# First weights in other buffers, w2 prepared sooner, and three statistics tied to the tile ahead of them, in a kernel of LayerNorm, Fourier mixing and MLP

## The chip, the cores and the metric

The kernel runs on one core of a Trainium2 chip. A core has a matrix engine (TensorE, PE in the profile), two elementwise engines (VectorE, DVE, and ScalarE, ACT), a slower general one (GpSimd, POOL) and a queue that issues transfers (SyncE, SP). PEld is TensorE's loading of weights, which runs beside its matmuls. The metric is the device time of one execution in microseconds; smaller is better. The time before is the median of three runs.

## The reference

```python
x = A_x                                    # (1, 2048, 576)
xn = _layernorm(x, axis=-1)
a = einsum("bsd,ed->bse", xn, dft_hid_re)
b = einsum("bsd,ed->bse", xn, dft_hid_im)
y = einsum("ts,bse->bte", dft_seq_re, a) - einsum("ts,bse->bte", dft_seq_im, b)
h = maximum(einsum("bsd,df->bsf", xn, w1), 0)      # w1: 576 x 4608
return x + y + einsum("bsf,fd->bsd", h, w2)        # w2: 4608 x 576
```

## The kernel before

All products are made from float16 halves: `split` (L164, L165) writes a high half on ScalarE (`hi = s * src`, rounded) and a low half on VectorE (`lo = s * src - hi`), and each product is a sum of three matmuls. The scale `s` is a power of two found from the largest magnitude: for w1 in `max_w1` (VectorE, L98) and `power_w1` (through TensorE, L140 and L148, with VectorE at L145 to L155), for w2 from sums of magnitudes that ScalarE makes in `sum_w2` (L375), and `power_w2`.

The 2048 rows of x are 16 tiles of 128 rows, in four groups g of four. The 4608 hidden columns of the MLP are nine blocks b of 512, each with two w1 halves (four parts f of 128 columns) and two w2 halves. A tile t goes through these steps: `stats([t])` takes mean and variance on VectorE (two L182, one L185, a square root on ScalarE at L192, then six small steps at L193 to L204); `normalize(t)`, N, writes the normalized tile on VectorE (L224) and its float16 form on ScalarE (L225); `remainder(t)`, E, subtracts the two (L229, L232), on VectorE for tile 0 and on GpSimd for the others; `transposes(t)`, T, makes nine transposes on TensorE (L240) and copies them out of PSUM on ScalarE into xT (L245, L248).

In the MLP `mlp1` and `tile_by` multiply xT by w1 (L286): `tile_by` for one tile of 128 rows and some parts f, `mlp1` for a group of four tiles. `mlp1_out` takes two such results through relu and makes sums and halves for a seven-product form of the second product (L303 to L314), with a temporary in a buffer tagged "stage" (two of them). `mlp2` makes one of the seven products with w2 (L328) and adds it to the accumulators on VectorE (L334). `sums_w2` (L405 to L408) and `split_w2` prepare w2.

The raw weights of all blocks lie in a pool "raw" of two buffers. At the start, SP issues tile 0 of x, the two w1 halves of block 0, x up to tile 7, then the two w2 halves, which have to wait until the w1 in their buffers is split, and then x of tiles 8 to 15 behind them.

The order in which an engine runs its instructions is not that of the source. It is fixed at compile time: the framework goes through the traced instructions with its own estimates of their times, prefers what stands earlier in the source, and takes something later when that is ready first. `tc.issue_after(ins)` ties that order: what is traced inside it for the engine of `ins` is put behind `ins` in that engine's queue, with no wait on a semaphore. `weave` runs a generator of steps and puts other calls between them. `fill(n)` traces n matmuls whose result nobody uses; they keep TensorE active.

Around the change, the source goes through block 0 for tiles 0 to 7 by hand: statistics of a tile, N, E, T, then `tile_by` for the parts of w1 that are split. The w2 of block 0 is summed, scaled and split between `tile_by(5)` and `mlp2`. After that a loop over blocks and groups runs `mlp1`, `mlp1_out` and the `mlp2` of the step before, with the preparation of the next block taken from a list.

Of the kernel before, what the change touches and what calls it, by code (L numbers as in the profile page):

```python
# [8 lines left out]
F16 = mybir.dt.float16  # L9
F32 = mybir.dt.float32  # L10
BF16 = mybir.dt.bfloat16
I32 = mybir.dt.int32
AF = mybir.ActivationFunctionType
# [28 lines left out]
def kernel(  # L42
# [41 lines left out]
        nc.sync.dma_start(r, src)  # L84

    def load_w1(b, i, parts=1):
        r = raws["w1", b, i] = raw.tile([P, 2 * KT, P], F32, tag="raw", name=f"raw_w1_{b}_{i}")
        n = 2 * KT // parts
        for k in range(0, 2 * KT, n):
            nc.sync.dma_start(r[:, k : k + n], w1[b, i][:, k : k + n])  # L90
# [70 lines left out]

    def split(hi, lo, src, s):

        nc.scalar.activation(hi, src, AF.Copy, scale=s)  # L164
        nc.vector.scalar_tensor_tensor(lo, src, s, hi, ALU.mult, ALU.subtract)  # L165


# [7 lines left out]
    def stats(ts):  # L175

        n = len(ts)
        mv = small.tile([P, n, 2], F32, tag=f"mv{n}", name=f"mv{ts[0]}")
        sts = [small.tile([P, 2, 6], F32, tag="st", name=f"st{t}", bufs=4) for t in ts]
        for t, st in zip(ts, sts):  # L180
            for j in range(2):
                nc.vector.bn_stats(st[:, j, :], acc[t][:, j * EH : (j + 1) * EH])  # L182
                yield
        for i, st in enumerate(sts):
            nc.vector.bn_aggr(mv[:, i], st.rearrange("p a b -> p (a b)"))  # L185
            yield
        r0, u, r, sh = (
            small.tile([P, n], F32, tag=f"{a}{n}", name=f"{a}_{ts[0]}") for a in ("r0", "u", "r", "sh")
        )
        m, v = mv[:, :, 0], mv[:, :, 1]  # L190
        stt = nc.vector.scalar_tensor_tensor
        nc.scalar.activation(u, v, AF.Sqrt, bias=eps)  # L192
        nc.vector.reciprocal(r0, u)  # L193
        yield

        stt(u, v, EPS, r0, ALU.add, ALU.mult)
        yield
        nc.vector.tensor_tensor(u, u, r0, ALU.mult)
        yield
        nc.vector.tensor_scalar(u, u, -0.5 * SX, 1.5 * SX, ALU.mult, ALU.add)  # L200
        yield
        nc.vector.tensor_tensor(r, u, r0, ALU.mult)
        yield
        stt(sh, m, -1.0, r, ALU.mult, ALU.mult)  # L204
        for i, t in enumerate(ts):
            means[t], factors[t], shifts[t] = mv[:, i, 0:1], r[:, i : i + 1], sh[:, i : i + 1]

    def weave(steps, *others):

        others = list(others)  # L210
        for _ in steps:
            if others:
                others.pop(0)()
        for f in others:
            f()
# [3 lines left out]
    def normalize(t, eng=nc.vector):  # L219
        stage = dpool.tile([P, 5 * EH], F32, tag="d", name=f"xn{t}")  # L220
        xn = xns[t] = stage[:, :D]

        xs = xss[t] = stage[:, D : 2 * D].bitcast(F16)
        eng.tensor_scalar(xn, acc[t], means[t], factors[t], ALU.subtract, ALU.mult)  # L224
        nc.scalar.activation(xs[:, :D], acc[t], AF.Identity, bias=shifts[t], scale=factors[t])  # L225

    def remainder(t, eng):
# [127 lines left out]
    def power_w1(b, i):  # L355
        s, p = (t["w1", b][:, i : i + 1] for t in (sc, pw))
        if b > 1:
            power(s, p, mx["w1", b][:, i : i + 1])
        else:
            power_pe(s, p, mx["b", i])  # L360

    def split_w1(b, f):
        i, r = divmod(f, 2)
        if r == 0:
            w1s[b, i] = mlp.tile([P, 2, 2 * KT, P], F16, tag="w1s", name=f"w1s{b}_{i}", bufs=4)
        w, k = w1s[b, i], slice(r * KT, (r + 1) * KT)
        split(w[:, 0, k], w[:, 1, k], raws["w1", b, i][:, k], sc["w1", b][:, i : i + 1])

    def sum_w2(b, i):

        if i == 0:
            mx["w2", b], sc["w2", b], pw["w2", b] = cell("mw2"), cell("tw2"), cell("pw2")
        junk = mlp.tile([P, 5, GH], F32, tag="stage", name=f"j{b}_{i}").rearrange("p a b -> p (a b)")
        junk = junk[:, : 4 * EH].rearrange("p (q e) -> p q e", e=EH)
        nc.scalar.activation(  # L375
            junk, raws["w2", b, i], AF.Abs, scale=2.0**-10, accum_out=mx["w2", b][:, i : i + 1]
        )
# [23 lines left out]
    def sums_w2(b, i):  # L401
# [5 lines left out]
        tt(b22, b22, b11, ALU.subtract)  # L407
        tt(b21, b21, b22, ALU.subtract)  # L408

    def split_w2(b, i, c):  # L410
        if c == 0:
            w2s[b, i] = mlp.tile([P, 2, 7, EH], F16, tag="w2s", name=f"w2s{b}_{i}", bufs=4)
        w, r = w2s[b, i], raws["w2", b, i]
        src = (r[:, 1:], r[:, :2], r[:, 2:])[c]
        q = (slice(B11, B22 + 1), slice(T3, T1 + 1), slice(T4, T2 + 1))[c]
        split(w[:, 0, q], w[:, 1, q], src, sc["w2", b][:, i : i + 1])
# [11 lines left out]
    def prepare_w2(b):  # L428
        steps = [lambda: sum_w2(b, 0), lambda: sum_w2(b, 1), lambda: power_w2(b)]
        steps += [lambda i=i: (split_w2(b, i, 0), sums_w2(b, i)) for i in range(NQ)]  # L430
        for i in range(NQ):
            steps += [lambda: None] * 2
            steps += [lambda i=i, c=c: split_w2(b, i, c) for c in (1, 2)]
        return steps
# [29 lines left out]
    def tile_by(t, fs, ps, wk=WK):  # L464
        g, c = divmod(t, TG)
        for i in fs:
            mlp1_group(0, g, i, slice(c * P, (c + 1) * P), ps[i], wk)

    no = lambda: None
    N, E, T = normalize, remainder, transposes  # L470

    def fill(n, src=idle):

        for _ in range(n):
            nc.tensor.matmul(ps[3][:, :256], src[:, :P], src[:, :256], start=True, stop=True)
# [5 lines left out]
    max_w1(0, 1)  # L481
    E(0, V)
    power_w1(0, 0)
    fill(14)
    T(0)
    fill(10, xss[0])
    split_w1(0, 0)
    tile_by(0, (0,), ps, WK0)
    split_w1(0, 1)
    tile_by(0, (1,), ps)  # L490
    weave(stats([1]))
    fill(8, xss[0])
    N(1)
    E(1, GP)
    T(1)
    fill(8, xss[1])
    s23 = stats([2, 3])
    weave(s23, no, lambda: max_w1(0, 2), no, lambda: max_w1(0, 3), lambda: power_w1(0, 1))
    tile_by(1, (0, 1), ps)
    split_w1(0, 2)  # L500
    N(2)
    E(2, GP)
    tile_by(0, (2,), ps)
    tile_by(1, (2,), ps)
    T(2)
    split_w1(0, 3)
    N(3)
    E(3, GP)
    tile_by(0, (3,), ps)
    tile_by(1, (3,), ps)  # L510
    T(3)
    tile_by(2, (0, 1, 2, 3), ps)
    weave(stats([4, 5, 6, 7]))
    for t in (4, 5, 6, 7):
        N(t)
        E(t, GP)
    T(4)
    tile_by(3, (0, 1, 2, 3), ps)
    pq = ps2.tile([P, 2, 512], F32, tag="ps2", name="p1_0_1")
    qs = [pq[:, 0], pq[:, 1]]  # L520
    T(5)
# [1 line left out]
    mlp1_out(0, 0, 0, *ps[:2])  # L523
    T(6)
    tile_by(5, (0, 1), qs)
    w = prepare_w2(0)
    w[0]()
    w[1]()
    w[2]()
    mlp1_out(0, 0, 1, *ps[2:])  # L530
    T(7)
    tile_by(6, (0, 1), qs)
    w[3]()
    tile_by(7, (0, 1), qs)
    w[4]()
    mlp1_out(0, 1, 0, *qs)
    for f in w[5:]:
        f()
# [322 lines left out]
```

## Time and profile before

| what | value |
|---|---|
| median of three runs | 1299.07 us (1297.1 to 1301.87) |
| the profiled execution | 1298.02 us |
| its span | 1296.2 us |
| TensorE busy | 1273.9 us (98%) |
| VectorE busy | 979.0 us (76%) |
| ScalarE busy | 532.0 us (41%) |
| GpSimd busy | 33.7 us (3%) |
| granted TensorE clock, mean | 0.997 |
| first matmul with w1 (L286) | at 11.81 us |
| first matmul with w2 (L328) | at 60.03 us |

The busy share of TensorE is an average that hides the start: in the first 60 us it is busy for 47.7 us, and some of that is `fill`. The granted clock is 1.00 but for a stretch in 17 to 24 us, where it is 0.50. A row of the timeline gives the start and the duration of an instruction, or of a run of like ones ("x9"), and in brackets how long the engine stood idle before it and what ended that.

### The profile page before, as it was taken

The page shows a single profiled execution, that of the slowest core. Times are in us where ns is not written, and L with a number is a line of the kernel's source. Part 1 is how long each engine was busy: PE and PEld are TensorE (multiplying, and loading weights), DVE is VectorE, ACT ScalarE, POOL GpSimd, SP SyncE. Part 2 cuts the span into 40 slices and gives each one's busy share as a digit, 9 for nine tenths or more (in the row PEclk, how much of TensorE's full clock was granted, in tenths as well). Part 3 has the DMA queues.
Part 4 walks back from the last instruction along what each step waited for, and adds up shares of the span by engine and source line. Part 5 has one row for each costly group of instructions (what it writes and reads, how often), then busy time and mean ns, then how long its engine had stood idle before and what let it go on. Part 6 is the DMA issues. An engine that isn't in the chain of part 4 may idle for free.

```text
span 1296.2 us, 21742 instructions
## 1 busy us (share of the span) xinstructions
PE 1273.9 (98%) x9106; PEld 873.0 (67%) x9106; DVE 979.0 (76%) x1671; ACT 532.0 (41%) x794; POOL 33.7 (3%) x60
## 2 busy tenths in 40 slices
PE   8799999999999999999999999999999999999998
PEld 6565666666666666666666556677777777777777
DVE  8978887596696685875866985567678887878875
ACT  4834444353443443443533432244443333333332
POOL 2210000000000000000000000000000000000000
PEclk8999999999999999999999999999999999999999
DMA  6102222122132131231221322330024435343420
GB/s 240 42 1 70 77 71 89 50 90 86 50 104 71 43 110 58 69 104 50 90 86 49 102 72 86 104 137 17 2 74 156 141 115 167 103 139 121 139 84 19
DMA packets 38002, 112.75 MB, mean 87 GB/s; under 512 B 3984, under 2 KB 10640, under 8 KB 37904
## 3 DMA queue, kind: packets, MB, share of 16 engines
q1 hardware_dynamic: 37904, 111.36, 25.8%
q8 instruction: 71, 1.16, 0.4%
q14 instruction: 27, 0.22, 0.1%
HBM read 101.91 MB, written 9.44 MB: 86 GB/s over the span
## 4 chain that ended last, share of the span: by engine, by line
PE 87%; DVE 6%; ACT 2%; DMA 2%; issue 1%; SPq 0%; POOLq 0%; POOL 0%; ACTq 0%; DVEq 0%
PE p L286 29%; PE p L795 25%; PE p L328 25%; PE pd L694 8%; DVE acc L334 1%; DMA raw_d<-in_dft_dram 1%; DVE w2s L165 1%; DVE h L307 0%; DVE c_md L98 0%; ACT xT L245 0%; DVE h L314 0%; DMA f<-in_cre_dram 0%; DVE xn L224 0%; ACT f L622 0%; ACT w2s L164 0%
## 5 line engine op out<-in xcount | busy, mean ns | idle before, releaser
L286 PE MATMUL p<-xT,w1s 128*128 128x512 f16 (+1 forms) x2268 | 462.6, 356 | 1.1 <-ACT xT L245 1.1
L328 PE MATMUL p<-w2s,h 128*128 128x288 f16 x3024 | 394.8, 286 | 3.4 <-DVE acc L334 2.9
L328 PEld LDWEIGHTS <-h 128*128 128x128 f16 x3024 | 295.2, 98 | 104.9 <-issue 4.6
L286 PEld LDWEIGHTS <-w1s 128*128 128x128 f16 x2268 | 209.1, 98 | 203.4 <-issue 1.9
L795 PE MATMUL p<-R,cs 128*128 128x288 f16 x2688 | 329.4, 286 | 0.0
L795 PEld LDWEIGHTS <-cs 128*128 128x128 f16 x2688 | 263.0, 98 | 66.3
L334 DVE SCALAR_TENSOR_TENSOR acc<-p,c_ub,acc 128x576 f32<-128x576 f32 x252 | 204.0, 812 | 17.6 <-PE p L328 17.2
L164 ACT ACTIVATE cs<-c,sc_c 128x1024 f16<-128x1024 f32 x112 | 128.6, 1148 | 201.3 <-PE p L795 149.5
L307 DVE SCALAR_TENSOR_TENSOR h<-p,h 128x256 f16<-128x256 f32 (+1 forms) x144 | 79.8, 556 | 135.6 <-ACT h L306 135.5
L165 DVE SCALAR_TENSOR_TENSOR cs<-c,sc_c,cs 128x1024 f16<-128x1024 f32 x112 | 143.7, 1283 | 49.9 <-ACT cs L164 49.7
L306 ACT ACTIVATE h<-p 128x256 f16<-128x256 f32 (+1 forms) x144 | 69.5, 484 | 221.6 <-PE p L286 219.3
L313 ACT ACTIVATE h<-s 128x1024 f16<-128x1024 f32 x72 | 76.1, 1057 | 170.8 <-DVE s L311 170.7
L694 PE MATMUL pd<-dsp,xT 128*128 128x288 f16 x896 | 109.9, 286 | 1.7 <-DVE acc L334 1.7
L314 DVE TENSOR_TENSOR h<-s,h 128x1024 f16<-128x1024 f32 x72 | 88.1, 1223 | 28.2 <-ACT h L313 28.1
L694 PEld LDWEIGHTS <-xT 128*128 128x128 f16 x896 | 87.7, 98 | 24.0 <-issue 1.9
L801 DVE SCALAR_TENSOR_TENSOR o<-p,us_c,o 128x288 f32<-128x288 f32 x112 | 57.5, 513 | 20.5 <-PE p L795 20.3
L622 ACT ACTIVATE f<-f 128x1024 f32<-128x1024 f32 x64 | 66.6, 1041 | 4.7 <-DMA f<-in_cre_dram 4.7
L164 ACT ACTIVATE w2s<-raw_w,c_sw 128x576 f16<-128x576 f32 (+1 forms) x54 | 43.9, 849 | 26.4 <-DVE c_sw L397 20.5
L165 DVE SCALAR_TENSOR_TENSOR w2s<-raw_w,c_sw,w2s 128x576 f16<-128x576 f32 (+1 forms) x54 | 46.6, 918 | 7.6 <-ACT w2s L164 7.6
L303 ACT ACTIVATE s<-p 128x256 f32<-128x256 f32 x72 | 26.6, 370 | 24.3 <-PE p L286 24.3
L712 ACT ACTIVATE R<-pd,c_rho 128x288 f16<-128x288 f32 x48 | 23.8, 499 | 21.8 <-DVE T L706 12.1
L165 DVE SCALAR_TENSOR_TENSOR w1s<-raw_w,c_sw,w1s 128x640 f16<-128x640 f32 x36 | 31.4, 892 | 0.0
(98 smaller groups left out, 633.0 us busy)
## 6 DMA issues: line engine op xcount, KB each, us to landing
f<-in_cre_dram SPq DMA_DIRECT2D x32, 512.0 KB, 3.5
f<-in_cim_dram SPq DMA_DIRECT2D x32, 512.0 KB, 3.5
c<-in_cre_dram SPq DMA_DIRECT2D x32, 512.0 KB, 4.1
c<-in_cim_dram SPq DMA_DIRECT2D x32, 512.0 KB, 4.6
raw_w<-in_w_dram SPq DMA_DIRECT2D x17, 640.0 KB, 4.1
raw_w<-in_w_dram SPq DMA_DIRECT2D x18, 576.0 KB, 4.0
acc<-in_x_dram SPq DMA_DIRECT2D x16, 288.0 KB, 6.4
spill<-acc SPq DMA_DIRECT2D x16, 288.0 KB, 2.5
```

What stands on the lines that cost most here:

```text
L164: nc.scalar.activation(hi, src, AF.Copy, scale=s)
L165: nc.vector.scalar_tensor_tensor(lo, src, s, hi, ALU.mult, ALU.subtract)
L286: nc.tensor.matmul(ps[:, cols], w1s[b, i // 2][:, hl, i % 2 * KT + k], xT[g][:, kx, cols], start=(n == 0), stop=(n == len(WK) - 1),)
L306: nc.scalar.activation(hi, src, AF.Relu)
L307: stt(lo, src, 0.0, hi, ALU.max, ALU.subtract)
L313: order["s"] = nc.scalar.activation(hi, st[:, 1:], AF.Copy).ins
L314: order["lo"] = nc.vector.tensor_tensor(lo, st[:, 1:], hi, ALU.subtract).ins
L328: nc.tensor.matmul(ps[:, c], h[:, x, qa, c * P : (c + 1) * P], w[:, y, qb], start=first and i == 0 and j == 0, stop=i == NQ - 1 and j == 2 ...
L334: nc.vector.scalar_tensor_tensor(o, ps, us[b], o, ALU.mult, ALU.add)
L622: nc.scalar.activation(f, f, AF.Abs, scale=2.0**-10, accum_out=sums_c[:, n, q : q + 1])
L694: nc.tensor.matmul(ps[j], xT[g][:, kx, c * P : (c + 1) * P], dsp[j][:, hl, k], start=(n == 0), stop=(n == len(XK) - 1),)
L795: nc.tensor.matmul(ps, w[:, a, k], r[:, c, rq], start=first and k == 0 and j == 0, stop=k == HK - 1 and j == 2, skip_group_check=not first,)
```

## The change

Seven edits, all of them about block 0 and tiles 0 to 7:

1. The raw w1 of block 0 goes into the two "stage" buffers, so that the two raw buffers are free for its w2 from the start.
2. For block 0 `sum_w2` writes its unused elementwise result into the buffer that the split w2 will have, instead of a "stage" buffer.
3. `split_w1(0, 0)` stands ahead of the first `fill(14)`, and the copies of T(0) are tied behind its high half on ScalarE (`order["hi"]`).
4. The statistics of tile 1 are tied behind N(0) on VectorE (`order["n"]`), and those of tiles 2 and 3, with the maxima and VectorE's part of the scale of w1's second half, behind N(1).
5. One `fill(8)` reads the low half of w1's part 1 in place of tile 0.
6. T(2) and the first two parts of `tile_by(2)` stand ahead of the split of w1's part 2; `split_w1(0, 2)`, N(3), T(3) follow.
7. The five first steps of `prepare_w2(0)` stand earlier: the two sums ahead of the statistics of tiles 4 to 7, scale and first split ahead of T(5), the second half's first split ahead of T(7).

```diff
     def load_w1(b, i, parts=1):
-        r = raws["w1", b, i] = raw.tile([P, 2 * KT, P], F32, tag="raw", name=f"raw_w1_{b}_{i}")
+        pool, tag = (raw, "raw") if b else (mlp, "stage")
+        r = raws["w1", b, i] = pool.tile([P, 2 * KT, P], F32, tag=tag, name=f"raw_w1_{b}_{i}")
...
-        nc.scalar.activation(hi, src, AF.Copy, scale=s)
+        order["hi"] = nc.scalar.activation(hi, src, AF.Copy, scale=s).ins
...
-        eng.tensor_scalar(xn, acc[t], means[t], factors[t], ALU.subtract, ALU.mult)
+        order["n"] = eng.tensor_scalar(
+            xn, acc[t], means[t], factors[t], ALU.subtract, ALU.mult
+        ).ins
...
-        junk = mlp.tile([P, 5, GH], F32, tag="stage", name=f"j{b}_{i}").rearrange("p a b -> p (a b)")
-        junk = junk[:, : 4 * EH].rearrange("p (q e) -> p q e", e=EH)
+        if b:
+            junk = mlp.tile([P, 5, GH], F32, tag="stage", name=f"j{b}_{i}")
+            junk = junk.rearrange("p a b -> p (a b)")[:, : 4 * EH]
+            junk = junk.rearrange("p (q e) -> p q e", e=EH)
+        else:
+            new_w2(b, i)
+            junk = w2s[b, i][:, 0, :4]
...
+    def new_w2(b, i):
+        w2s[b, i] = mlp.tile([P, 2, 7, EH], F16, tag="w2s", name=f"w2s{b}_{i}", bufs=4)
...
-        if c == 0:
-            w2s[b, i] = mlp.tile([P, 2, 7, EH], F16, tag="w2s", name=f"w2s{b}_{i}", bufs=4)
+        if b and c == 0:
+            new_w2(b, i)
...
-    no = lambda: None
+    no, after = lambda: None, lambda: tc.issue_after(order["n"])
...
     power_w1(0, 0)
+    split_w1(0, 0)
     fill(14)
-    T(0)
+    with tc.issue_after(order["hi"]):
+        T(0)
     fill(10, xss[0])
-    split_w1(0, 0)
     tile_by(0, (0,), ps, WK0)
     split_w1(0, 1)
     tile_by(0, (1,), ps)
-    weave(stats([1]))
-    fill(8, xss[0])
+    with after():
+        weave(stats([1]))
+    fill(8, w1s[0, 0][:, 1, KT:].rearrange("p k f -> p (k f)"))
     N(1)
     E(1, GP)
     T(1)
     fill(8, xss[1])
-    s23 = stats([2, 3])
-    weave(s23, no, lambda: max_w1(0, 2), no, lambda: max_w1(0, 3), lambda: power_w1(0, 1))
     tile_by(1, (0, 1), ps)
-    split_w1(0, 2)
+    with after():
+        s23 = stats([2, 3])
+        weave(s23, no, lambda: max_w1(0, 2), no, lambda: max_w1(0, 3), lambda: power_w1(0, 1))
     N(2)
     E(2, GP)
+    T(2)
+    tile_by(2, (0, 1), ps)
+    split_w1(0, 2)
+    N(3)
+    E(3, GP)
     tile_by(0, (2,), ps)
     tile_by(1, (2,), ps)
-    T(2)
     split_w1(0, 3)
-    N(3)
-    E(3, GP)
+    T(3)
     tile_by(0, (3,), ps)
     tile_by(1, (3,), ps)
-    T(3)
-    tile_by(2, (0, 1, 2, 3), ps)
+    w = prepare_w2(0)
+    w[0]()
+    w[1]()
     weave(stats([4, 5, 6, 7]))
     for t in (4, 5, 6, 7):
         N(t)
         E(t, GP)
+    tile_by(2, (2, 3), ps)
     T(4)
     tile_by(3, (0, 1, 2, 3), ps)
+    w[2]()
+    w[3]()
...
     T(6)
     tile_by(5, (0, 1), qs)
-    w = prepare_w2(0)
-    w[0]()
-    w[1]()
-    w[2]()
     mlp1_out(0, 0, 1, *ps[2:])
+    w[4]()
     T(7)
     tile_by(6, (0, 1), qs)
-    w[3]()
     tile_by(7, (0, 1), qs)
-    w[4]()
     mlp1_out(0, 1, 0, *qs)
```

## The prediction

> **What bounds the kernel now.** I read the page's engine shares first, then a table by stage, then the queues in order of time. The page: TensorE is busy in 1273.9 of 1296.2 us and the 40 slices show nines from the third slice on, so whatever can be won lies in the first 60 us, where this change is. Stage table of ten microseconds (columns: stretch, its length, busy time and instruction count of each engine, granted clock, DMA share, GB/s):
>
> ```profile
> 10.00:20.00 10.00, 6.92 (x72) 5.16 (x70) 9.28 (x34) 4.35 (x9) 1.42 (x2) 0.85 0.92 333
> 20.00:30.00 10.00, 10.00 (x143) 9.40 (x142) 9.81 (x33) 5.50 (x9) 2.96 (x5) 0.81 0.48 177
> 30.00:40.00 10.00, 7.91 (x140) 7.62 (x137) 7.46 (x21) 9.61 (x20) 5.97 (x8) 1.00 0.01 2
> 40.00:50.00 10.00, 8.01 (x107) 6.32 (x105) 9.63 (x21) 9.12 (x15) 4.39 (x6) 1.00 0.01 2
> 50.00:60.00 10.00, 5.90 (x47) 3.31 (x45) 10.00 (x20) 8.89 (x17) 1.76 (x2) 1.00 0.02 2
> ```
>
> See that TensorE is not the limit there. VectorE is full in 10 to 30 and 40 to 60; ScalarE is half empty in 10 to 30 and full afterwards. From 60 us on TensorE has work almost without a break, so every microsecond by which it gets there sooner comes off the end.
>
> Next, VectorE in order of time (columns: start, duration, engine, line, operation, tiles). This is the chain from the square root of tile 1 to its normalized tile:
>
> ```profile
> 12.43 0.15 DVE L193 RECIPROCAL r<-u 128x1 f32<-128x1 f32 x1
> 12.49 0.80 DVE L98 TENSOR_REDUCE c_mf<-raw_w 128x1 f32<-128x640 f32 x1
> 13.21 0.15 DVE L196 SCALAR_TENSOR_TENSOR u<-mv,r 128x1 f32<-128x1 f32 x1
> 13.27 0.46 DVE L182 BATCH_NORM_STATS2 st<-acc 128x6 f32<-128x288 f32 x1
> 13.64 0.15 DVE L198 TENSOR_TENSOR u<-u,r 128x1 f32<-128x1 f32 x1
> 13.70 0.46 DVE L182 BATCH_NORM_STATS2 st<-acc 128x6 f32<-128x288 f32 x1
> 14.07 0.14 DVE L200 TENSOR_SCALAR u<-u 128x1 f32<-128x1 f32 x1
> 14.12 0.82 DVE L98 TENSOR_REDUCE c_mf<-raw_w 128x1 f32<-128x640 f32 x1
> ...
> 15.12 0.58 DVE L224 TENSOR_SCALAR xn<-acc,mv,r 128x576 f32<-128x576 f32 x1
> ```
>
> Steps of 0.15 us stand behind work of other tiles that the planned order put between them. TensorE in the same stretch, then its clock, from a table of two microseconds (columns as above):
>
> ```profile
> 16.16 0.63 PE L240 MATMUL pt<-ident,xn 128*128 128x128 f16 x5 [2.52 <-ACT xn L225]
> ...
> 19.28 0.27 PE L140 MATMUL pm<-ident,mb 128*1 128x128 bf16 x1
> ...
> 23.81 3.30 PE L286 MATMUL p<-xT,w1s 128*128 128x128 f16 x56
> ```
>
> ```profile
> 14.00:16.00 2.00, 0.00 (x0) 0.00 (x0) 2.00 (x10) 0.76 (x1) 0.00 (x0) 1.00 0.96 369
> 16.00:18.00 2.00, 1.28 (x12) 0.82 (x13) 2.00 (x8) 0.30 (x2) 1.42 (x2) 0.75 1.01 357
> 18.00:20.00 2.00, 2.00 (x15) 1.29 (x13) 1.28 (x8) 1.19 (x2) 0.00 (x0) 0.50 1.03 389
> 20.00:22.00 2.00, 2.00 (x20) 1.79 (x19) 1.85 (x8) 1.29 (x2) 0.34 (x2) 0.50 1.06 410
> ```
>
> TensorE stands still for 2.52 us until tile 1 is normalized, and is then granted half its clock from 17 to about 23.8 us. Last, the later half: ScalarE's sums over w2 and the gap that they cause, from the two queues in order of time:
>
> ```profile
> 34.81 1.18 ACT L375 ACTIVATE j<-raw_w 128x1152 f32<-128x1152 f32 x1
> ...
> 36.44 1.19 ACT L375 ACTIVATE j<-raw_w 128x1152 f32<-128x1152 f32 x1
> ...
> 37.58 1.05 ACT L245 ACTIVATE xT<-pt 128x1024 f16<-128x1024 f16 x1
> ...
> 38.85 0.66 PE L240 MATMUL pt<-ident,xn 128*128 128x128 f16 x9 [1.39 <-ACT xT L248]
> ```
>
> **The change, part by part.** Sums are against the profiled execution, 1298.02 us (span 1296.2 and 1.82 around it); the median of the three runs, 1299.07, is 1.05 above it.
>
> Statistics of tile 1 behind N(0). VectorE waits 0.61 us for x1 at 7.52 with the first half of these statistics, then spends 0.38 on it, while the last steps of tile 0 stand behind. Without that, L202 starts at 6.92 instead of 7.90 and N(0) at about 7.2 instead of 8.22. The w1 scale gains only the second half at 8.78 (0.37): the matmul for it still follows the idle matmuls, which end at 7.5. So the split of w1 starts near 9.0 (9.31 before). The first real matmul, 11.81, waits for the copies of xT(0), which stood behind both halves of that split. The new edge puts them behind the first half: 10.8 if the second goes behind them, 11.5 if it goes ahead. But then the second half ends as late as before or 0.5 us later, and the group for f=1 with it. I take 0.3 us, on the square root of tile 1 (11.82 before); ends 0 and 0.9.
>
> Statistics of tiles 2 and 3, max_w1(0,2), max_w1(0,3) behind N(1). By the rows above they take 0.72+0.37+0.37+0.73 and 0.14 of aggregation out of that chain: 2.3 us. Bare, the chain's six steps take 0.19 each (the same steps run so at 73.36 to 74.03 us), so N(1) starts at 13.0. But tiles 4 to 7 are not ordered: their statistics came directly behind those of tile 3 (15.73), and their x are issued by 6.76 and land in a median 6.4. Four of them in the gaps (0.37 each) put N(1) at 14.5. I take 13.7, the middle, since nothing says how many are planned as ready; ends 13.0 and 14.5 against 15.12.
>
> What is queued behind that: the four statistics (1.5 us), both maxima (1.5) and aggregation (0.3), so the second scale's matmul can start at 13.7+0.5+3.3=17.5. It ran at 19.28, since it stood in TensorE's queue behind T(1). From there to the first w1 low half for f=2 it took 4.5 us (19.28 to 23.8), so the full stretch that began at 23.81 begins at 22.0 to 22.6. If the matmul is planned behind tile_by(1), which the source now puts first, it comes at about 19.4 and nothing is won here. I take 1.3 us; ends 0 and 2.
>
> The clock. 28 matmuls at half clock took 3.35 us (0.82+2.53), 28 at full clock 1.72 (at 11.81); T(2) took 1.17 instead of 0.66. These 2.1 us are no extra gain: TensorE then waited 0.24 for w1's low half, which the term above already moves. The new filler, eight matmuls of 0.12 us (1.47 for 12), now needs the low half for f=1 and so falls into the 2.52 us of standstill: it costs nothing, since the second part of T(1) waits for POOL (0.31+1.15) in any case. Without that cover it costs 1 us.
>
> Moved groups: tile_by(2, f 0 and 1) needs no second split and bridges the wait for it; T(2), T(3), N(3) keep their counts (9 transposes, 1.3 us of copies, 1.45 on POOL). Zero, between a loss of 0.8 (one wait for POOL as at 31.87, 0.70, planned wrongly) and a gain of the same.
>
> Buffers and loads. w1 in the stage buffers is let go with the last split, 24.55; the first user of the buffer is at 34.29, so 9.7 us of cover. Both w2 loads are issued near 7 instead of 12.17 and 24.58, and SP no longer stands before x8 to x15. The 1.18 MB take 3.1 us of DMA at 380 GB/s, behind x0 to x7; x8 is first read at 24.47, after some 19. The first load of f (18.28) moves up and has no user before. Loads of the next block's w1 (58.99) follow the last w2 split and are first read at 84.71. All zero. Summing into the w2 operand writes f16 instead of f32: 864 elements to f16 took 0.96, 1152 to f32 1.18, so the same per element within 0.1 us.
>
> The w2 sums. 2 x (1.18+0.22)=2.8 us leave ScalarE's full stretch for its gaps at 16.3 (2.0), 19.5 (1.2), 23.0 (0.9) and 26.0 (2.9). The gap of 1.39 us ahead of T(6) goes. The scaling of w2 (some 3 us on VectorE between 38.72 and 47.6) and its first split (1.07, and four differences of 0.42) can then use VectorE's one large hole, 2.36 us ahead of 33.36. Late next are the same copies: gaps of 0.85, 1.05, 0.9, 1.75 and 1.45 us ahead of 60 us remain where ScalarE and VectorE are full. Ends 1.4 (only that gap) and 2.8 (all of ScalarE's relief); I take 2.0, since VectorE, full from 40 on, gets only its hole. Against it: a sum of 1.4 planned just ahead of a critical copy; ends 0 and 1.4 twice, I take 0.3.
>
> Sum: 1.3+2.0-0.3=3.0 us (the 0.3 of tile 1 is inside the 1.3). 1298.02-3.0=1295.0.
>
> **The rivals.** First, the engines are the limit and the order gives nothing: VectorE is 19.6 of 20 busy in 40 to 60, and what is moved is not removed. For it: 53.9 us of VectorE work in the first 60. Against: the 2.36 hole and ScalarE's. 1298, from 1296.5 to 1300.
>
> Second, more than summed: every standstill of VectorE up to 80 us goes, 2.3 ahead of 10, 0.9 to 30, 2.5 to 40, 2.8 after, 8.5 us: 1289.5. Against it: the first 3.67 us wait for x0, and some idle always remains.
>
> Third, slower, one mechanism: the clock is halved in a stretch that is full. A window with TensorE mostly idle cost 6.8 us at half clock, in a stretch with slack. If the second scale comes late while tile_by(1) is done early, TensorE stands from 19.4 to 22.8, and 6.8 us at half clock cover the full stretch from 23.8: half of it, 3.4 us, is lost, and it decides once the rest gains less than 3.4. With nothing else won 1301.4; with a second halving in 40 to 60, where the gaps are, 1304.8, with a third 1308.2. Against it: tile_by(2, f 0 and 1) bridges, and stretches with 5.9 of 10 busy kept the full clock.
>
> [...]
>
> **How the numbers follow.** Forecast, 1292.6 to 1296.5: 0.42. Engines the limit: 0.23. More than summed, below 1292.6: 0.18. Half clock: 0.17, of it 0.08 beyond 1305.6. One half percent is 6.5 us, about what a measurement of this kernel can tell from no change. Faster 0.18, same 0.74, slower 0.08. The range reaches to 1288.5 (the second rival with 1 us of scatter) and to 1303 (the third with one halving and the scatter of the runs); the forecast's own is 1292.6 to 1296.5.
>
> **What would show it.** Right: N(1) near 13.7, the second scale's matmul near 17.5, no clock of 0.5 in 18 to 22, the w2 sums ahead of 30 us, no gap of 1.4 us ahead of T(6), the first matmul of L328 near 57 instead of 60.03. Wrong: statistics of tiles 4 to 7 between the steps of tile 1; the second scale's matmul behind tile_by(1); the clock at 0.5 later than 24; gaps before T(9) to T(11) grown by what T(6) gave.

## The result, and the profile after

| | before | after |
|---|---|---|
| median, six runs each on one chip | 1299.35 us (1297.1 to 1301.87) | 1304.01 us (1303.69 to 1305.95) |
| the profiled execution | 1298.02 us | 1305.13 us |
| its span | 1296.2 us | 1303.3 us |
| TensorE busy | 1273.9 us | 1276.1 us |
| granted clock, mean | 0.997 | 0.994 |
| first matmul with w2 | at 60.03 us | at 66.68 us |

The ratio is 1.0038, 95% interval [1.0025, 1.0051]: slower by 4.7 us, against a forecast of 1295.0 and a range up to 1303.0. The loss is below the half percent that was taken as the bound of what can be told, but the interval lies wholly above 1. The two profiled executions lie 7.1 us apart in span, 2.4 more than the medians: before's is among its quicker ones and after's among its slower ones.

Two points of time divide the start. M1 is the end of the first 224 real matmuls (`tile_by` of tiles 0 to 3), M2 the end of the 28 matmuls of 128x512 that follow the first matmuls with w2 (12 of these before, seven after). M1 is at 35.40 us before and at 40.48 after, M2 at 67.71 and 75.34. So 5.1 us are lost by 40 us and 2.5 between 40 and 75, together 7.6; behind M2 0.5 of it comes back. The stage table of after shows both places (columns: stretch, its length, busy time and instruction count of PE, PEld, DVE, ACT, POOL, granted clock, DMA share, GB/s):

```profile
10.00:20.00 10.00, 6.96 (x85) 5.46 (x83) 8.02 (x27) 5.62 (x9) 1.43 (x2) 1.00 1.04 399
20.00:30.00 10.00, 5.13 (x55) 4.39 (x52) 8.40 (x31) 6.14 (x12) 3.81 (x4) 0.78 0.33 124
30.00:40.00 10.00, 9.87 (x156) 9.70 (x154) 5.89 (x22) 6.01 (x11) 4.53 (x8) 0.88 0.01 2
40.00:50.00 10.00, 6.76 (x114) 6.26 (x112) 9.60 (x26) 8.49 (x14) 3.47 (x5) 1.00 0.01 2
50.00:60.00 10.00, 8.97 (x85) 5.65 (x83) 10.00 (x20) 9.28 (x18) 1.11 (x1) 1.00 0.01 2
60.00:70.00 10.00, 6.24 (x34) 3.41 (x32) 6.83 (x12) 5.54 (x8) 2.97 (x4) 0.66 0.42 132
```

In 20 to 30, where TensorE was busy throughout before, it is busy for half; and the clock, low there and in 30 to 40, is low a second time in 60 to 70. VectorE's holes in 10 to 40 have grown (8.02, 8.40 and 5.89 us busy, 9.28, 9.81 and 7.46 before): it waits there more than it did.

TensorE of after in order of time (columns here and below: start, duration, engine, line, operation, tiles, count, and in brackets the idle time ahead and what ended it):

```profile
19.12 1.72 PE L289 MATMUL p<-xT,w1s 128*128 128x128 f16 x28 [0.46 <-ACT xT L248]
20.77 0.22 PE L141 MATMUL pm<-ident,mb 128*1 128x128 bf16 x1
21.36 0.16 PE L149 MATMUL pm<-top,ones 1*128 1x1 bf16 x1 [0.37 <-DVE top L146]
24.62 0.23 PE L289 MATMUL p<-xT,w1s 128*128 128x128 f16 x1 [3.10 <-DVE w1s L166]
...
27.60 5.31 PE L289 MATMUL p<-xT,w1s 128*128 128x128 f16 x51
...
33.25 3.29 PE L289 MATMUL p<-xT,w1s 128*128 128x128 f16 x56
```

The second scale's matmul (L141) stands behind all 28 matmuls of `tile_by(1)`. Then TensorE has nothing for 3.10 us, until the low half for f=2 is there, and the 51 matmuls that follow take 5.31 us; at the rate of the last row they would take 3.0. The clock in steps of two microseconds:

```profile
22.00:24.00 2.00, 0.00 (x0) 0.00 (x0) 2.00 (x10) 1.67 (x3) 0.00 (x0) 1.00 0.56 219
24.00:26.00 2.00, 0.47 (x5) 0.29 (x5) 2.00 (x6) 1.39 (x2) 1.29 (x2) 0.90 0.02 6
26.00:28.00 2.00, 1.51 (x13) 1.25 (x14) 2.00 (x7) 0.16 (x1) 2.00 (x4) 0.50 0.00 0
28.00:30.00 2.00, 2.00 (x22) 2.00 (x20) 0.99 (x5) 1.22 (x3) 0.52 (x1) 0.50 0.00 0
```

Half the clock is granted from 25.6 to 32.4 us. The 5.1 us at M1 then add up: the full stretch begins at 27.60 instead of 23.81 (3.79), the clock costs 5.31-3.0=2.3, and 1.0 comes back, since five of the matmuls (0.3) are already done and the 0.70 us that TensorE waited for GpSimd at 31.87 before is not there.

Why the low half is late stands in VectorE's queue:

```profile
14.01 0.16 DVE L194 RECIPROCAL r<-u 128x1 f32<-128x1 f32 x1
...
15.05 0.58 DVE L225 TENSOR_SCALAR xn<-acc,mv,r 128x576 f32<-128x576 f32 x1
15.54 0.81 DVE L183 BATCH_NORM_STATS2 st<-acc 128x6 f32<-128x288 f32 x2
16.27 0.81 DVE L99 TENSOR_REDUCE c_mf<-raw_w 128x1 f32<-128x640 f32 x1
...
18.62 0.11 DVE L356 TENSOR_REDUCE mb<-c_mf 128x1 bf16<-128x2 f32 x1
18.64 1.18 DVE L183 BATCH_NORM_STATS2 st<-acc 128x6 f32<-128x288 f32 x3
20.59 0.17 DVE L194 RECIPROCAL r<-u 128x2 f32<-128x2 f32 x1 [0.78 <-ACT u L193]
...
22.17 0.12 DVE L152 TENSOR_SCALAR c_sw<-half 128x1 int32<-128x1 int32 x1
...
23.21 0.56 DVE L225 TENSOR_SCALAR xn<-acc,mv,r 128x576 f32<-128x576 f32 x1
23.70 0.86 DVE L166 SCALAR_TENSOR_TENSOR w1s<-raw_w,c_sw,w1s 128x640 f16<-128x640 f32 x1
```

N(1) runs at 15.05 (15.12 before). All that was tied behind it, the four statistics and two maxima, comes only then, so that the second scale's input (mb) is made at 18.62 (15.03 before) and the scale itself (c_sw) at 22.17 (21.08 before); eight halves of the statistics of tiles 4 to 7 are planned into the waits and steps of that chain, and N(2) runs at 23.21 instead of 20.59.

Between 40 and 75 us, TensorE's queue:

```profile
44.00 0.16 PE L149 MATMUL pm<-top,ones 1*128 1x2 bf16 x1 [2.71 <-DVE top L146]
...
63.68 0.71 PE L243 MATMUL pt<-ident,xn 128*128 128x128 f16 x5 [2.71 <-POOL xn L232]
...
68.31 7.03 PE L289 MATMUL p<-xT,w1s 128*128 128x512 f16 x28
```

The 1.39 us ahead of T(6) are gone. In their place TensorE waits 2.71 us for VectorE's `top` (L146) of the w2 scale, whose small matmul L149 is now in its queue ahead of `tile_by(4)`, and 2.71 us for tile 10, as VectorE's queue shows:

```profile
59.81 1.53 DVE L166 SCALAR_TENSOR_TENSOR w2s<-raw_w,c_sw,w2s 128x576 f16<-128x576 f32 x2
...
62.40 1.06 DVE L225 TENSOR_SCALAR xn<-acc,mv,r 128x576 f32<-128x576 f32 x2
```

N(10) and N(11) run at 62.40, behind the splits of w2; before, N(11) ran at 45.93, ahead of them. The 28 matmuls after that take 7.03 us instead of 6.21, at half clock until 70.0.

### The profile page after: what moved, and what is told of

Its sections match the earlier page's. It is cut to its first block, busy times and chain, and to the rows that moved or that the text cites. A ratio compares the mean times of both kernels' runs of the same rounds, so it can differ in the third digit from the quotient of the medians.

```text
span 1303.3 us, 21740 instructions
## 1 busy us (share of the span) xinstructions
PE 1276.1 (98%) x9106; PEld 874.2 (67%) x9106; DVE 976.7 (75%) x1671; ACT 532.5 (41%) x794; POOL 34.2 (3%) x60
## 4 chain that ended last, share of the span: by engine, by line
PE 88%; DVE 6%; DMA 2%; ACT 2%; issue 1%; POOL 0%; SPq 0%; POOLq 0%; ACTq 0%; DVEq 0%
PE p L289 29%; PE p L810 25%; PE p L331 25%; PE pd L709 8%; DVE acc L337 1%; DMA raw_d<-in_dft_dram 1%; DVE w2s L166 1%; DMA raw_w<-in_w_dram 1%; DVE h L310 0%; DVE h L317 0%; DVE c_md L99 0%; DMA f<-in_cre_dram 0%; POOL xn L235 0%; ACT xn L228 0%; ACT f L637 0%
## 5 line engine op out<-in xcount | busy, mean ns | idle before, releaser
L727 ACT ACTIVATE R<-pd,c_rho 128x288 f16<-128x288 f32 x48 | 23.8, 499 | 21.9 <-DVE T L721 12.1
```

## The experiments

Theory A: the ties behind N(1) are the cause. They hold back the second scale and tiles 2 and 3 and open the standstill at 21.5. Theory B, the main rival: the sums over w2 are the cause, which now stand at 19.1 and 20.5 in ScalarE's queue ahead of and behind the square root of tiles 2 and 3. A further question is what the half clock itself costs. Edits are numbered as in the section on the change; the lines shown are against the changed kernel unless another is named, "..." standing for arguments left as they are. The runs of before that each is compared with are those of its own chip job.

**Without ties (edit 4 undone).**

```diff
-    with after():
-        weave(stats([1]))
+    weave(stats([1]))
...
-    with after():
-        s23 = stats([2, 3])
-        weave(s23, ...)
+    s23 = stats([2, 3])
+    weave(s23, ...)
```

> The changed kernel without the ties of the statistics of tiles 1 to 3 (edit 4); all else kept. Theory A (the ties make the scale of w1's second half and N(2) late, TensorE stands 3.1 us and then runs 6.8 us at half clock): the matmul for the second scale comes before 20 us, the standstill ahead of T(2) shrinks below 1.5 us, no half clock in 26 to 32 us, time 1297 to 1300. Theory B (the earlier w2 work on ScalarE and VectorE delays the chain, not the ties): the square root of tiles 2 and 3 still stands behind a sum over w2, time 1302 to 1305.

Measured 1297.3 us, ratio 0.9993 [0.9985, 1.0002]. The loss is gone. Its TensorE:

```profile
18.64 0.22 PE L141 MATMUL pm<-ident,mb 128*1 128x128 bf16 x1
...
19.32 1.74 PE L289 MATMUL p<-xT,w1s 128*128 128x128 f16 x28
21.35 0.61 PE L243 MATMUL pt<-ident,xn 128*128 128x128 f16 x5 [0.29 <-ACT xn L228]
...
45.15 3.19 PE L289 MATMUL p<-xT,w1s 128*128 128x512 f16 x14
...
55.72 0.45 PE L243 MATMUL pt<-ident,xn 128*128 128x128 f16 x5 [2.71 <-POOL xn L232]
```

The second scale's matmul goes ahead of `tile_by(1)`, which then bridges the wait, and T(2) follows at 21.35. The 14 matmuls of 128x512 end at 48.34, and at 51.09 before: 2.75 us ahead, about what the prediction summed (3.0), though without the ties from which 1.3 of it was to come. Then tile 10 comes late, as in after, and the half clock falls on what follows (57.2 to 64.0 us); M2 is at 68.34, behind before's 67.71, with five matmuls of w2 fewer done by then.

**w2 late (edit 7 undone, ties kept).** `prepare_w2(0)` and its first five steps go back to where they were before.

```diff
-    w = prepare_w2(0)
-    w[0]()
-    w[1]()
     weave(stats([4, 5, 6, 7]))
...
     tile_by(5, (0, 1), qs)
+    w = prepare_w2(0)
+    w[0]()
+    w[1]()
+    w[2]()
     mlp1_out(0, 0, 1, *ps[2:])
```

> The changed kernel with the sums, scale and first splits of w2 back at their old places in the source (edit 7 undone); all else kept. Theory A: the second scale still comes after 20 us and the first standstill and the half clock at 26 to 32 us stay; only the stretch from 55 us gains, time 1300 to 1303. Theory B: the square root of tiles 2 and 3 comes 1.3 us sooner, N(10) and N(11) are done before 55 us instead of 62.4, both half clock stretches go, time 1297 to 1299.

Measured 1304.16 us, 1.0044 [1.0032, 1.0056], M1 at 40.24. The standstill is 3.10 us as in after. Theory B falls for the first standstill. The gain from 55 us on that theory A expected did not come either: the wait ahead of T(6) is 2.20 us, and the clock is halved again at 45.3 and 65.7.

**Bridge.** Idle matmuls for the time of the standstill.

```diff
         weave(s23, no, lambda: max_w1(0, 2), no, lambda: max_w1(0, 3), lambda: power_w1(0, 1))
+    fill(28, xss[1])
     N(2)
```

> The changed kernel with 28 more idle matmuls, from the operand of tile 1, traced behind the second scale, so that TensorE does not stand still ahead of T(2). Theory C (the half clock after the standstill is a cost of its own): no granted clock of 0.5 in 26 to 32 us, and 51 matmuls that took 5.3 us take 3.0, so 2 to 3 us gained: 1301 to 1302. If the half clock lies in slack that the engines' chain would wait for in any case: time as changed, 1303 to 1305.

Measured 1303.48 us, 1.0039 [1.0027, 1.0052]: no gain that stands clear of the interval (some 1.6 us either way). Yet it does what it should. From its TensorE queue:

```profile
20.52 2.36 PE L486 MATMUL p<-xn 128*128 128x256 f16 x20
23.60 0.23 PE L289 MATMUL p<-xT,w1s 128*128 128x128 f16 x1 [0.73 <-DVE w1s L166]
```

And from its table by stage:

```profile
24.00:28.00 4.00, 2.19 (x34) 1.84 (x33) 3.22 (x10) 1.75 (x4) 3.49 (x4) 1.00 0.00 0
...
42.00:44.00 2.00, 2.00 (x25) 2.00 (x22) 2.00 (x10) 1.21 (x2) 0.00 (x0) 0.54 0.00 0
...
64.00:68.00 4.00, 4.00 (x15) 1.88 (x14) 1.62 (x3) 2.14 (x3) 0.00 (x0) 0.50 0.02 4
```

The clock stays whole after 24 us, and M1 is at 37.30, 3.2 us sooner than in after, of which 1.0 is a luckier start (w1's second half landed without a wait: N(1) at 14.01). The clock is halved at 42.2, right behind the same wait of 2.71 us for the w2 scale, and at 62.6. That the filler moved a halving to 42.2 is not shown, since the run with the old start has both without this filler: 51 matmuls at 27.07 in 4.44 us (3.0 at whole clock) and 28 at 43.01 in 2.54 (1.72). The lateness of N(2) remains (22.18, and 20.59 before).

**w2 alone.** The kernel before with edits 1, 2 and 7.

```diff
     tile_by(3, (0, 1, 2, 3), ps)
+    w[2]()
+    w[3]()
...
     mlp1_out(0, 0, 1, *ps[2:])
+    w[4]()
     T(7)
```

> The kernel before with only the buffers and the earlier w2 (edits 1, 2 and 7): no ties, old start, old order of the tile groups. Theory A: faster or as before, 1295 to 1299, with the gap ahead of T(6) gone. Theory B: slower than before, 1301 to 1304, with N(10) and N(11) after 58 us.

Measured 1300.51 us, 1.0017 [1.0009, 1.0026]. With the buffers alone beside it, the earlier w2 costs 2 us: the small matmul L149 waits 3.11 us in TensorE's queue, and tiles 10 and 11 wait behind the splits (2.62 us ahead of T(10)).

**Tie of tile 1 only.** The tie behind N(1) is taken away, that behind N(0) stays.

```diff
-    with after():
-        s23 = stats([2, 3])
-        weave(s23, ...)
+    s23 = stats([2, 3])
+    weave(s23, ...)
```

> The changed kernel with the tie of tile 1's statistics kept and the ties of tiles 2 and 3, both maxima and the second scale behind N(1) taken away. If the ties behind N(1) are what made the second scale and N(2) late: the second scale's matmul comes before 20 us, no standstill of 3 us ahead of T(2), time as without any tie, 1296 to 1299. If the tie of tile 1 is as much to blame: the standstill stays and the time is 1301 to 1304.

Measured 1297.59 us, 0.9994 [0.9985, 1.0003]: the same as without both. The tie behind N(0) costs nothing and brings nothing that can be told; the tie behind N(1) carries the loss. Theory A holds. Whether the tie behind N(1) costs as much without the one behind N(0), and which of the instructions tied by it (four statistics, two maxima, the scale) is the dear one, was not tried. The traces point at the statistics of tiles 2 and 3. From VectorE's queue in this run, N(2) and the low halves for f=2 and 3:

```profile
19.70 0.57 DVE L225 TENSOR_SCALAR xn<-acc,mv,r 128x576 f32<-128x576 f32 x1
...
26.14 1.62 DVE L166 SCALAR_TENSOR_TENSOR w1s<-raw_w,c_sw,w1s 128x640 f16<-128x640 f32 x2
```

And from TensorE's:

```profile
24.93 1.73 PE L289 MATMUL p<-xT,w1s 128*128 128x128 f16 x28
27.02 4.86 PE L289 MATMUL p<-xT,w1s 128*128 128x128 f16 x84 [0.36 <-DVE w1s L166]
```

The low half for f=2 comes later here than in after (26.14 against 23.70), and so do N(1) (16.80 against 15.05) and the scale (23.37 against 22.17), yet TensorE waits for it only 0.36 us: N(2) is early, so T(2) and `tile_by(2)` do bridge the wait.

**Ties alone.** The kernel before with edit 4 and nothing else.

```diff
+        order["n"] = eng.tensor_scalar(...).ins
...
+    with tc.issue_after(order["n"]):
+        weave(stats([1]))
...
+    with tc.issue_after(order["n"]):
+        weave(s23, ...)
```

> The kernel before with nothing but the two ties (edit 4), so with the copies of T(0) behind both halves of the first split as before. If the ties cost only together with the new start (edit 3), which puts tile 1's square root behind the second half of the split: N(1) comes at 13.0 to 13.7, the second scale's matmul before 18.5, time 1296 to 1299. If the ties cost by themselves: N(2) after 22 us, time 1301 to 1304.

Measured 1300.47 us, 1.0008 [0.9999, 1.0016]. The medians are 2.0 us apart. So the ties need company to cost 5 us. Here the standstill is 1.92 us and no half clock follows it in the profiled run. That run is one of four with a mean granted clock of 0.999; the other seven have 0.996, so they were at half clock for longer, and where is not on record.

**Without ties, w2 late (edits 1, 2, 3, 5 and 6).** Both edits shown above for those two runs.

> The changed kernel without the ties and with the w2 work at its old places: both suspects gone, buffers, start and tile groups of the change kept. Without the ties alone the kernel was 3 us ahead of the one before at 45 us and lost it to N(10) and N(11), which come only after 53 us behind the w2 splits. Theory D (these late tiles cost 3 to 4 us): here N(11) is done before 48 us, no standstill of 2.7 us ahead of T(10), time 1294 to 1297; but the gap of 1.4 us ahead of T(6) is back, so not below 1294. If the w2 work costs nothing: 1297 to 1298 as without the ties alone.

Measured 1298.11 us, 0.9995 [0.9986, 1.0003]. The hope for 1294 to 1297 failed: the gaps ahead of the transposes (1.69, 1.43, 1.45) are those of before.

**Tiles 8 to 11 first.** No ties; w2 is summed and scaled early, but its splits stay where they were before, and tiles 8 to 11 come ahead of them.

```diff
     tile_by(3, (0, 1, 2, 3), ps)
     w[2]()
-    w[3]()
...
-    w[4]()
     T(7)
+    weave(stats([8, 9, 10, 11]))
+    for t in (8, 9, 10, 11):
+        N(t)
+        E(t, GP)
     tile_by(6, (0, 1), qs)
+    w[3]()
     tile_by(7, (0, 1), qs)
+    w[4]()
```

> The changed kernel without the ties, with the sums and the scale of w2 early as in the change, the two first splits of w2 back behind tile_by(6) and tile_by(7), and the statistics, N and E of tiles 8 to 11 moved ahead of them, behind T(7). Theory D: N(10) and N(11) come before 48 us, T(10) and T(11) stand behind no wait of 2.7 us, mlp2 starts near 57 us, time 1292.5 to 1295.5. If the w2 splits, now later, hold up mlp2 instead: it starts at 60 us or later and the time is 1297 to 1300.

Measured 1295.21 us, 0.9972 [0.9960, 0.9984]: faster than both kernels. From its TensorE queue:

```profile
37.10 0.16 PE L149 MATMUL pm<-top,ones 1*128 1x2 bf16 x1 [0.50 <-DVE top L146]
...
55.65 1.17 PE L243 MATMUL pt<-ident,xn 128*128 128x128 f16 x18 [0.42 <-ACT xT L251]
58.72 1.02 PE L331 MATMUL p<-w2s,h 128*128 128x288 f16 x7 [1.91 <-ACT xT L251]
```

The wait for tile 10 is gone and that for the w2 scale is 0.50 us (1.02 and 0.50 already in the runs without ties and with the tie of tile 1 only), the first matmul with w2 comes at 58.72, M2 at 65.83. These are 3 us, as much as the prediction looked for, but without the ties that were to bring part of it, and with two obstacles removed that it had not priced.

**Old group order (edit 6 undone, ties kept).** Shown in part:

```diff
+    tile_by(1, (0, 1), ps)
+    split_w1(0, 2)
     N(2)
     E(2, GP)
-    T(2)
-    tile_by(2, (0, 1), ps)
-    split_w1(0, 2)
-    N(3)
-    E(3, GP)
     tile_by(0, (2,), ps)
     tile_by(1, (2,), ps)
+    T(2)
```

> The changed kernel with the tile groups in the order of before (edit 6 undone), the ties kept. With the ties alone on the kernel before, N(2) was as late (22.8 us) and the time only 1 us longer; there all 28 matmuls of f=2 stood ahead of T(2), in the change only one did, and T(2) waited behind it for the second split. If this place in TensorE's queue is what the ties cost together with edit 6: time 1299 to 1301. If not: 1303 to 1305.

Measured 1302.22 us, 1.0033 [1.0021, 1.0045]; standstill 2.34 us. By the times of its matmuls the clock is halved behind the standstill (28 at 24.22 in 3.04 us, 1.73 at whole clock; the nine transposes at 27.10 take 0.67 again) and from 58.1 at the latest to about 68 (nine transposes in 1.14 to 1.20 us, and the 28 of 128x512 at 67.07 in 6.65 instead of 6.2).

**Old start (edit 3 undone, ties kept).**

```diff
-    split_w1(0, 0)
     fill(14)
-    with tc.issue_after(order["hi"]):
-        T(0)
+    T(0)
     fill(10, xss[0])
+    split_w1(0, 0)
```

> The changed kernel with the old start (edit 3 undone): the split of w1 and the copies of T(0) in their old places, ties and group order of the change kept. If the new start (tile 1's square root behind the second half of the split, VectorE idle 0.71 and 0.91 us ahead of the low halves) is what the ties cost together with: N(1) before 14 us, standstill ahead of T(2) below 2 us, time 1298 to 1301. If the cost is the place of the work behind N(1): time as changed, 1303 to 1305.

Measured 1304.46 us, 1.0049 [1.0036, 1.0062]; standstill 3.10. Undoing 3, 6 or 7 singly cures nothing.

**Ties with tiles 8 to 11 first.** The ties are put back into the fastest kernel.

> The changed kernel, ties kept, with the two first splits of w2 back and the statistics, N and E of tiles 8 to 11 ahead of them, as in the fastest kernel so far. If the two losses are separate (ties ahead of 30 us, late tiles after 50 us): the standstill ahead of T(2) stays, that ahead of T(10) goes, and 2.5 to 4 us are gained on the change: 1300 to 1301.5. If the late tiles cost nothing once the first loss is there: 1303 to 1305.

Measured 1303.22 us, 1.0037 [1.0024, 1.0050], standstill 3.10, and half the clock behind it (the 51 matmuls at 26.37 take 5.36 us; 3.0 at whole clock). Against the same kernel without ties that is 8 us, from one edit: what was gained by 60 us is not there to be gained when the ties have delayed everything ahead of it.

**Fastest with filler.** Tiles 8 to 11 first, with 18 more idle matmuls around T(1).

```diff
+    fill(10, xss[0])
     T(1)
     fill(8, xss[1])
+    fill(16, xss[1])
```

> The fastest kernel so far (no ties, tiles 8 to 11 first) with 18 more idle matmuls around T(1), ten ahead of it and eight behind. In that kernel's profile 56 matmuls at 23.9 us took 4.87 us, partly at half clock, where 3.29 is usual. If the half clock there costs what it takes: no clock of 0.5 ahead of 30 us and 1 to 1.6 us less, 1293.5 to 1294.5. If it lies in slack or comes and goes between runs: 1295 to 1296.

Measured 1295.97 us, 0.9986 [0.9977, 0.9995]: no gain over the kernel without it. The halving at 23.8 is gone (28 matmuls at 23.46 in 1.73 us), and one behind 58.45 is there (28 of 128x512 in 7.89 us, 6.20 in the kernel without the filler).

It was still open which company makes the ties dear. Four runs add the other edits one at a time to the ties, against the kernel before.

**Ties with buffers (edits 1, 2, 4, 5), and with edit 3, edit 6 or edit 7 added.** Each is the changed kernel with the undoings above of what it leaves out (for the first: 3, 6 and 7).

> The kernel before with edits 1, 2, 4 and 5 (buffers, both ties, the filler's operand), without edits 3, 6 and 7. With edit 4 alone the ratio was 1.0008, with all seven 1.0038, and undoing any single one of 3, 6 and 7 cured nothing. If the earlier loads in the changed buffers are what makes the ties dear (the second half of w1 or x then lands otherwise): 1.003 or more, standstill near 3 us ahead of T(2). If an edit of the order is needed: 1.000 to 1.0015, standstill 1.9 to 2.4.

> As the run with buffers and ties, with edit 3 added (split of w1's first part ahead, copies of T(0) behind it). If the later first matmul (12.35 instead of 11.81) shifts the standstill by 0.5 us and nothing else: 1.001 to 1.002. If edit 3 with the ties is enough for the whole loss: 1.0035 to 1.0045.

> As the run with buffers and ties, with edit 6 added (T(2), tile_by(2) ahead of the split of w1's part 2). If the split of part 2 behind N(2) makes the standstill long: standstill 3 us, clock halved from about 24 us, 1.0035 to 1.005. If edit 6 is harmless, as it bridges the wait: 1.000 to 1.0015.

> As the run with buffers and ties, with edit 7 added (w2 summed, scaled and split sooner). Edit 7 without the ties cost 0.0017, the ties alone 0.0008. If the two only add up: 1.0025. If the sum over w2 ahead of the square roots of tiles 2 and 3 on ScalarE makes the standstill longer: 1.0035 or more and half clock from 24 us.

The last column is from the one profiled execution of each.

| edits | ratio [95%] | standstill | clock just after it |
|---|---|---|---|
| 4 | 1.0008 [0.9999, 1.0016] | 1.92 us | whole |
| 1, 2, 4, 5 | 1.0027 [1.0017, 1.0036] | 2.34 us | half |
| 1, 2, 4, 5 and 3 | 1.0016 [1.0008, 1.0025] | 2.34 us | whole |
| 1, 2, 4, 5 and 7 | 1.0031 [1.0020, 1.0042] | 2.34 us | half |
| 1, 2, 4, 5 and 6 | 1.0043 [1.0030, 1.0055] | 3.10 us | half |
| all seven | 1.0038 [1.0025, 1.0051] | 3.10 us | half |

The row of TensorE that ends the standstill, with the ties alone:

```profile
22.86 1.74 PE L288 MATMUL p<-xT,w1s 128*128 128x128 f16 x28 [1.92 <-DVE w1s L165]
```

With the buffers:

```profile
23.34 2.88 PE L289 MATMUL p<-xT,w1s 128*128 128x128 f16 x28 [2.34 <-DVE w1s L166]
```

With edit 3 added to the buffers:

```profile
23.48 1.74 PE L289 MATMUL p<-xT,w1s 128*128 128x128 f16 x28 [2.34 <-DVE w1s L166]
```

With edit 6 added, and the second scale's matmul:

```profile
20.14 0.22 PE L141 MATMUL pm<-ident,mb 128*1 128x128 bf16 x1
...
23.98 0.23 PE L289 MATMUL p<-xT,w1s 128*128 128x128 f16 x1 [3.10 <-DVE w1s L166]
```

The buffers lengthen the standstill by 0.42 us: VectorE runs six halves of later statistics between the scale's input and the first low half, where it ran five, and one half moves it on by 0.43. Edit 6 lengthens it by 0.76: the second scale's matmul goes behind all 28 matmuls of `tile_by(1)` instead of behind 11 of them (20.14; 19.52 with the buffers only), eight halves stand in the chain instead of six, and N(2) stands ahead of the low half.

With the runs further up, each of edits 3, 6 and 7 is now seen with and without each of the others, always with 1, 2, 4 and 5. Edit 6 adds 0.0016, 0.0028, 0.0018 and 0.0005 (1.0027 to 1.0043 with neither of the others; 1.0016 to 1.0044 with 3; 1.0031 to 1.0049 with 7; 1.0033 to 1.0038 with both), in the mean 0.0017 or 2.2 us. Edit 3 changes the ratio by -0.0011, +0.0001, +0.0002 and -0.0011, edit 7 by +0.0004, +0.0017, +0.0006 and -0.0006: both within the intervals. So the ties become dear with the buffers (0.0019 by these ratios, 0.0014 by the plain means of the runs of the two jobs) and with edit 6 (0.0017). That the buffers act through earlier planned loads is inferred; which edit of 1, 2 and 5 it is was not tried.

## Why the prediction was wrong

**What bounds the start.** Right: the time is decided in the first 70 us, and TensorE is not the limit there.

**Statistics of tile 1 behind N(0).** The step put N(0) at 7.2 and the first real matmul at 10.8 to 11.5; they came at 8.18 and 12.35. Two causes. VectorE waited 1.03 us at 6.80 for the second half of the raw w1, a wait that before's profile doesn't have; where it was absent (the bridge) N(0) ran at 7.13, so this part was right but for the landing. And E(0), 0.8 us, with half of tile 1's statistics now stood ahead of the first scale's last steps: c_sw at 10.40, 9.15 before. The prediction named both places for the second half of the split but no such delay of the scale. By the run with this tie alone, the edit is worth nothing that can be told either way.

**Ties behind N(1).** The step that failed. It counted 2.3 us of work taken out of tile 1's chain and placed N(1) at 13.7. The chain did run bare, 0.19 a step as foretold, but from 14.01, so N(1) came at 15.05. The square root was done at 13.36 (13.07 and 0.29), but w1's second low half, which waits for ScalarE's high half (12.35 and 0.83), stands at 13.21 ahead of the chain in VectorE's queue. VectorE stood idle for 0.71 and 0.91 us ahead of the two low halves; with the tie of tile 1 only, statistics and a maximum fill these waits. So the work was not removed from the path; it was moved out of waits that cost nothing to a place where the second scale and tiles 2 and 3 wait for it. "Nothing is won" if the scale's matmul is planned behind `tile_by(1)`, at about 19.4, was the pessimistic end of the term. It was planned there, at 20.77, and the end should have been a loss: N(2) late by 2.6 us, and the full stretch by 3.8, where the term had a gain of 1.3.

**Clock.** "No extra gain" was right, and so was the third rival: TensorE was to stand from 19.4 to 22.8 and stood from 21.5 to 24.6; 6.8 us of half clock were to cover the stretch from 23.8 and covered 25.6 to 32.4. Its 1301.4 with one halving and 1304.8 with two stand beside the measured 1304.01 with two. That nearness is in part luck, as its price was made up otherwise: the first halving cost 2.3 us, not 3.4, as T(2) waited for GpSimd in a part of it, and the lateness of N(2) and the low half, which the rival left at zero, made up the other 2.8 us of M1. The bridge took the first halving away and the end stayed within the interval, with others at 42.2 and 62.6. A price at the end can be read from the runs of before beside the experiments: their mean time is 1296.9 us at a mean granted clock of 1.000 (10 runs), 1297.6 at 0.999 (33), 1298.8 at 0.997 (38) and 1301.0 at 0.995 (4), by estimate from these means some 1 us for each 3.41 us at half clock (half of the 6.83 measured in before and after, and 0.0013 of the mean clock). At one clock, 0.996, before took 1299.9 us (3 runs) and the bridge 1303.3 (5), so some 3 us of the loss are there at an equal share of half clock. What else differed between these runs is not known. What spoke against this rival, that `tile_by(2)` bridges, failed because T(2) needs N(2), which stands ahead of the low half in the same late chain: only one matmul ran before it. Where N(2) was early, at 19.70 with the tie of tile 1 only, it did bridge.

**Moved groups, buffers: zero.** True without ties (0.9995 with edits 1, 2, 3, 5 and 6). With the ties, edit 6 costs some 2 us and the buffers as much. The zeros were worked out singly; what they share is one chain of VectorE. The new filler was free, as said: it ended at 15.99, and the float16 form of tile 1 that T(1) waits for at 16.04.

**The w2 sums.** The gap ahead of T(6) went, as foretold. The term missed what follows the sums: the scale's matmul in TensorE's queue (2.71 us, and 1.02 without the ties, where the term expected VectorE's hole to take the scaling) and N(10), N(11) behind the splits. Gained 2.0 by the prediction, w2 alone loses 2 (1.0017). With the scale early, the splits late and tiles 8 to 11 first, the mechanism pays.

As to the gaps ahead of a halving: 3.10 us ahead of T(2) were followed by one each time (five runs), 2.34 us in three of four runs (those of the table and the old group order), and 1.92 us, once, by none. The length alone does not settle it, for the 2.71 us ahead of 44.0 in after were followed by whole clock (28 matmuls in 1.72 us).

## What to carry to other kernels

Work that filled the waits of a chain cost nothing here that can be told (0.9994 with the tie of tile 1 only, where it fills them, against 1.0038 in after); before such work is tied behind the chain, count who waits for the work itself, and price the late end of that, not only the chain that gets free. A small matmul of a scale held up all that stood behind it in TensorE's queue until its operand was there (2.71 us ahead of 44.0 in after, 3.11 with w2 alone), so an earlier preparation must be followed through each of its steps, not only through the engine that it frees. A filler against the clock's halving gained nothing that can be told in the two runs that tried it: in both, the clock was halved at another place.

## What the runs showed of the hardware

The halvings last 3.41 us or a multiple of it, as far as the tables of the clock show their ends: 6.83 us at 17.0 of before and at 25.6 and 63.1 of after, 3.4 at 23.8 in the fastest kernel, 10.2 from 57.8 in the run with the buffers. The stretch at whole clock between the two halvings of after, 30.72, is a multiple too. Whether a gap halves the clock is not settled by its length: 2.34 us did so with the buffers, and not with edit 3 added, as the two rows above show (28 matmuls in 2.88 and 1.74 us). The 2.52 us ahead of T(1) halved it before; in the run with w2 alone 2.51 us at the same place didn't (its next 28 matmuls took 1.74 us, 3.35 in before). The fastest kernel and the one without ties have the same gaps to 0.03 us from 16 to 24, and only in one of the two profiles, that of the fastest, is the clock halved there (at 23.8, with no gap over 0.9 us since 17). So like gaps ended differently, and no run shows what decides it.

VectorE's steps of 128x4 took 0.2 us, and two of them 1.1. From VectorE's queue in after, in the chain of tiles 8 to 11:

```profile
38.33 0.23 DVE L199 TENSOR_TENSOR u<-u,r 128x4 f32<-128x4 f32 x1
38.59 1.09 DVE L201 TENSOR_SCALAR u<-u 128x4 f32<-128x4 f32 x1
```

GpSimd's queue at that time:

```profile
38.50 1.16 POOL L235 TENSOR_TENSOR xn<-xn 128x512 f16<-128x512 f32 x1
```

The step that begins within GpSimd's subtraction ends when that ends (39.68 and 39.66), and the same happens again with the step at 39.97 (1.08) beside the subtraction at 39.88 (1.15). Both stand ahead of the `top` for which TensorE waits at 44.0. A chain of small steps beside GpSimd's remainders can so be longer by nearly the whole of one of its instructions at a time.
